# Spectral filter and SwiGLU on one core: the first filter load on SyncE, early fillers, a filter table of 33 slots, and another order of squares and sums

## The chip, the cores and the metric

The kernel runs on one core of one Trainium2 chip. Its time is the device time of one execution in microseconds; a kernel's time is the median over its runs. TensorE multiplies, VectorE and ScalarE (ACT) empty its PSUM banks, GpSimd (POOL) does elementwise work and issues DMAs, and SyncE (SP) only issues DMAs.

## The reference

```
X = rfft(x, axis=1)                    # x: 8 x 3008 x 256, along the 3008
Y = X * (filt_r + 1j * filt_i)         # 1505 frequencies x 256 channels
t = irfft(Y, n=3008, axis=1)           # 24064 tokens x 256
tn = t / sqrt(mean(t*t, -1) + 1e-6) * rms_g
g, val = tn @ w_gate, tn @ w_val       # 256 -> 1536
out = (g * sigmoid(g) * val) @ w_out   # 1536 -> 256
```
All inputs and the output are float32.

## The kernel before

**The transform.** 3008 is 47 x 64, so a transform is two stages of matmuls with constant tables: stage A over the 64 (table `wa`), stage B over the 47 (`wb`, one 96x96 block for each of 32 values of k2). The filter is multiplied in between B and its inverse (`wi`), and the inverse of A (`wai`) follows. Then each token is normed and goes through the gated layer: `gv` (gate and value, L545; Silu on ACT, product `hh` on VectorE) and `down` (L562).

**The filter table.** `ff` holds for each half `dh` of the channels and each k2 three sections of 48: minus imaginary, imaginary, real. The filters arrive in three loads of 512 rows (`f_load(i)`, filt_i as f=0 and filt_r as f=1, 512 KB each, on POOL's queue). `f_unit(i, f, dh, e)` transposes four 128x128 f32 blocks on TensorE (L390) and copies them into `ff` on engine `e`: 8 of 16 frequencies in rising k2, the other 8 mirrored, in four copies, because the mirror of k2=0 falls into another row. `f_neg(k0, n)` makes the minus section on POOL (L408) for both halves.

**The prologue, batch 0.** It is written out by hand, and each engine takes its instructions in the order written. `x_load(0, c)` are four loads on POOL; wa, ident, idf, wai and three tiny tails go on SyncE. `a0_unit` is stage A for four rows and one channel half (L359; psum on bank 1 for dh=0, emptied by ACT, bank 2 for dh=1, emptied by VectorE). `fill(n)` issues n matmuls on zeros whose result nobody reads (L425). `tr0_unit(g)` transposes stage A's result back (L369), eight times. Then a loop over 16 units (four k2 and one channel half each, unit i = 2g + dh) does stage B: `b_unit` (L243) and the two products `s_part` on VectorE (e=0 with the real section, L233; e=1 with the other two, L236), `yt0_unit` (sums the two products and transposes them on TensorE, L417, emptied by ACT), `bi_unit` (stage B's inverse, L287, emptied by ACT into `uu`, L197). After it `t4_load` moves `uu` by four transposing DMAs on SyncE (L301), `first_norm` norms the first tokens, and `n_first(1)` norms the second four rows from t4's first two chunks (L482).

POOL's queue in that time is: x(0), the filters, wb, wi, the weight loads `w_load(0)`, `w_load(1)`, then f_neg and `w_load(2)`, `wo_load`, the loads of x(1) and `w_gain` (weights times rms_g) in turn. `bank(i)` gives psum tiles: 0 is `mx` (one buffer), 1 `pg` and 2 `pv` (two buffers each, shared with gv), 3 `mb` (one buffer).

**The steady part.** 576 items (8 batches x 6 groups of rows x 12 blocks of 128 columns) each take one slot: `gv` of the slot, the planned units, `down` of the item two slots back. A planner places the units of the next batches: `a_unit` (stage A, bank 0 or 3, L208), `b_unit`, `s_part`, `add_unit` (sum of the products on POOL, L270), `yt_load` (transposing DMA, L277), `bi_unit`, `t4_load`, `n_unit` (L316), `sq_unit` (two squares with sums on ACT, L324), `stat_unit` and `xt_unit` (POOL, L332 to L342), `tr_unit` (transposing DMA). `fit` moves a unit to the first slot where its bank is free and ACT and VectorE have room by fixed costs. Within a slot units stand in the order in which they were planned, but what is in `front` is put first:

```python
        front = (sq_unit, s_part)
        def at(slot, fn, *a):
            todo = (late if fn == q_unit else plan).setdefault(slot, [])
            if fn in front:
                todo.insert(0, (fn, a))
            else:
                todo.append((fn, a))
```

Of the kernel before, what the change touches and what calls it, by code (L numbers as in the profile page):

```python
# [10 lines left out]
FP32 = mybir.dt.float32  # L11
# [9 lines left out]
P = 128  # L21
D = 256
# [3 lines left out]
H = 24  # L26
K2 = 32
SL = 48
# [6 lines left out]
NXC = H // XC  # L35
# [65 lines left out]
def kernel(  # L101
# [11 lines left out]
    nc = tc.nc  # L113
# [7 lines left out]
    if_d = nc.inline_tensor(if_np, name="if_t").ap()  # L121
# [3 lines left out]
    glob = ctx.enter_context(tc.tile_pool(name="glob", bufs=1))  # L125
# [25 lines left out]
    uu = glob.tile([P, H, 2, P], FP16)  # L151
    left = glob.tile([P, 2, K2, 2], FP16)
    va = uu.rearrange("p c e t -> p (c e t)").rearrange("p (e k j) -> p e k j", e=2, k=K2)
    ff = glob.tile([P, 2, K2, 3 * SL], FP32)
    wg = glob.tile([P, 2, DFF], FP16)
    wv = glob.tile([P, 2, DFF], FP16)
    wo = glob.tile([P, JT, D], FP16)
# [18 lines left out]
    def x_load(b, c):  # L176
        t = xp.tile([P, XC, D], FP16, tag="xc", name="xc")
        row = b * N + c * XC
        src = lambda n, w, lo=0: raw(x.flatten_outer_dims(), row + lo, [[N1 * D, n], [H * D, 2], [1, w * D]])
        if b == B - 1 and c == NXC - 1:  # L180
            w = XC - 1
            nc.vector.memset(t[96:P, w, :], 0.0)
            nc.gpsimd.dma_start(t[:, 0:w, :].rearrange("p a d -> p (a d)"), src(N2, w))
            nc.gpsimd.dma_start(t[0:P - 2, w, :], src(N2 - 1, 1, w))
            nc.gpsimd.dma_start(t[P - 2:P - 1, w, :],
                                raw(x.flatten_outer_dims(), row + w + (N2 - 1) * N1, [[D, 1], [1, D]]))
        else:
            nc.gpsimd.dma_start(t.rearrange("p a d -> p (a d)"), src(N2, XC))
        st[b]["x"][c] = t
# [5 lines left out]
    def copy(eng, out, in_, scale=None):  # L195
        if eng == "A":
            nc.scalar.activation(out=out, in_=in_, func=AXT.Copy, **({} if scale is None else {"scale": scale}))  # L197
        elif scale is None:
            nc.vector.tensor_copy(out=out, in_=in_)
        else:  # L200
            nc.vector.tensor_scalar(out=out, in0=in_, scalar1=scale, scalar2=None, op0=ALU.mult)
# [36 lines left out]
    def b_unit(b, i, bk=3):  # L238
        g, dh = divmod(i, 2)
        ps = bank(bk, "psb")[:, 0:4 * KR]  # L240
        for k in range(4):
            kk = 4 * g + k
            nc.tensor.matmul(ps[:, ts(k, KR)], st[b]["t2"][kk // KC][:, kk % KC, ds(dh * P, P)],  # L243
                             wb[0:KR, kk, :], start=True, stop=True)
        s = [sp.tile([P, 4, KR], FP16, tag="s%d" % e, name="s%d" % e) for e in range(2)]
        st[b]["s"][i] = (ps.rearrange("p (k r q) -> p k r q", k=4, r=2), s)
        s_part(b, i, 0)
# [127 lines left out]
    fst = {}  # L375
    FR4 = 4

    def f_load(i):
        t = stg.tile([P, 2, FR4, D], FP32, tag="stg", name="fs")
        fst[i] = t  # L380
        row = FR4 * P * i if i < 2 else NF - 1 - FR4 * P
        for f, src in ((0, filt_i), (1, filt_r)):
            nc.gpsimd.dma_start(t[:, f].rearrange("p a d -> p (a d)"),
                                raw(src, row, [[FR4 * D, P], [1, FR4 * D]]))

    def f_unit(i, f, dh, e):
        t = fst[i]
        ps = bank(1 + "AV".index(e), "psf").rearrange("p (a q) -> p a q", a=FR4)
        for a in range(FR4):
            nc.tensor.transpose(ps[:, a, :], t[:, f, a, ds(dh * P, P)], idf)  # L390
        v = ps.rearrange("p a (q s) -> p s a q", s=16)
        fk = ff[:, dh].rearrange("p (t k) c -> p t k c", k=4)
        lo = SL * (1 + f) + 8 * i
        hi = lo + H
        if i < 2:
            copy(e, fk[:, :, :, lo:lo + 8], v[:, 0:8])
            copy(e, fk[:, ::-1, 1:4, hi:hi + 8][:, :, ::-1, :], v[:, 8:16, 1:4, :])
            copy(e, fk[:, 1:8, 0, hi:hi + 8][:, ::-1, :], v[:, 9:16, 0, :])
            copy(e, ff[:, dh, 0, hi:hi + 8], v[:, 8, 0, :])
        else:  # L400
            copy(e, fk[:, :, :, lo:lo + 8], v[:, 8:16])
            copy(e, fk[:, ::-1, 1:4, hi:hi + 7][:, :, ::-1, :], v[:, 0:8, 1:4, 1:8])
            copy(e, fk[:, 1:8, 0, hi:hi + 7][:, ::-1, :], v[:, 1:8, 0, 1:8])
            copy(e, ff[:, dh, 0, hi:hi + 7], v[:, 0, 0, 1:8])

    def f_neg(k0, n):
        for dh in range(2):
            nc.gpsimd.tensor_scalar(out=ff[:, dh, k0:k0 + n, 0:SL], in0=ff[:, dh, k0:k0 + n, SL:2 * SL],  # L408
                                    scalar1=-1.0, scalar2=1.0, op0=ALU.mult, op1=ALU.mult)

# [11 lines left out]
    def fill(n, bk=0):  # L422
        ps = bank(bk, "pf")
        for _ in range(n):
            nc.tensor.matmul(ps, wa, ss3[0].rearrange("p k e q -> p (k e q)")[:, 0:512], start=True, stop=True)  # L425

    def t4_first():
        t = xtp.tile([P, 4, D], FP16, tag="xt", name="t4f")
# [160 lines left out]
    def w_load(q):  # L589
        cols = ts(q, DFF // 3)  # L590
        t = stg.tile([P, 2, 2, DFF // 3], FP32, tag="stg", name="ws")
        for src, k in ((moe_w_gate, 0), (moe_w_val, 1)):
            nc.gpsimd.dma_start(t[:, k], src.rearrange("(dt p) j -> p dt j", p=P)[:, :, cols])
        wst[q] = t

    def wo_load(q):
        nc.gpsimd.dma_start(wo[:, ts(q, JT // 3), :],
                            moe_w_out.rearrange("(jt p) d -> p jt d", p=P)[:, ts(q, JT // 3), :])

    def w_gain(q):  # L600
        cols = ts(q, DFF // 3)
        t = wst.pop(q)
        for k, dst in enumerate((wg, wv)):
            for dt_ in range(2):
                nc.gpsimd.tensor_scalar(out=dst[:, dt_, cols], in0=t[:, k, dt_, :],
                                        scalar1=gsb[:, dt_:dt_ + 1], scalar2=1.0,
                                        op0=ALU.mult, op1=ALU.mult)

    with tc.manual_schedule():
        nc.vector.memset(mhalf, -0.5)  # L610
        nc.vector.memset(epsb, 1e-6 * Y_SCALE * Y_SCALE)
        nc.scalar.activation(out=warm, in_=epsb.to_broadcast([P, 4]), func=AXT.Sqrt)
        for c in range(NXC):
            x_load(0, c)
        nc.sync.dma_start(wa, wa_d)
        nc.sync.dma_start(ident, id_d)
        nc.sync.dma_start(idf, if_d)
        nc.sync.dma_start(wai, wai_d)
        tail = op.tile([P, 4, D], FP32, tag="o3", name="tail")
        for f, src in ((0, filt_i), (1, filt_r)):  # L620
            nc.sync.dma_start(tail[0:1, f, :], raw(src, NF - 1, [[D, 1], [1, D]]))
        nc.sync.dma_start(tail[0:2, 2, 0:P], moe_rms_g.rearrange("(a p) -> a p", p=P))
        for i in range(3):
            f_load(i)
        for h in range(2):
            nc.gpsimd.dma_start(wb[:, ts(h, K2 // 2), :], wb_d[:, ts(h, K2 // 2), :])
        nc.gpsimd.dma_start(wi, wi_d)
        w_load(0)
        w_load(1)
        nc.vector.memset(ones, 1.0)  # L630
        for t in ss3:
            nc.vector.memset(t, 0.0)
        nc.vector.memset(ff.rearrange("p e k (s q) -> p e k s q", s=3)[:, :, 1:K2, :, SL - 1], 0.0)

# [2 lines left out]
        def a0(*gqs):  # L637
            for gq in gqs:
                for dh in range(2):
                    a0_unit(gq, dh, E[dh], 1 + dh)  # L640

        a0(0)
        fill(2)
        a0(1, 2)
        psg = bank(3, "psg")
        for f in range(2):
# [5 lines left out]
        copy("V", gsb, psg[:, 4:6])  # L652
        fill(2)
        a0(3)
        fill(1)
        a0(4, 5)
        todo = [(i, f, dh) for i in range(2) for f in range(2) for dh in range(2)]
        todo += [(2, f, dh) for dh in range(2) for f in range(2)]
        f_unit(*todo[0], "A")
        f_unit(*todo[1], "A")  # L660
        for g in range(8):
            tr0_unit(g, "V")
            if g < 7:
                f_unit(*todo[g + 2], "A")
        for n, u in enumerate(todo[9:]):
            f_unit(*u, "VAA"[n])
        f_neg(0, 8)
        w_load(2)
        f_neg(8, 8)
        wo_load(0)  # L670
        f_neg(16, 16)
        wo_load(1)
        wo_load(2)
        for c in range(NXC):
            x_load(1, c)
        for q in range(3):
            w_gain(q)
        UN = K2 // 2
        for p in range(UN + 3):
            if p < UN:  # L680
                b_unit(0, p, (0, 3)[p % 2])
                s_part(0, p, 1)
            if 2 <= p < UN + 1:
                yt0_unit(p - 2, "A", 1)
            if p == UN + 1:
                yt0_unit(UN - 1, "V", 1, slice(0, 2))
                yt0_unit(UN - 1, "A", 0, slice(2, 4))
            if 4 <= p < UN + 3:
                bi_unit(0, p - 4, "AV"[p == UN + 1], 2)
            if UN + 1 <= p < UN + 3:  # L690
                fill(1, 1)
        bi_unit(0, UN - 1, "V", 3, slice(0, 2))
# [6 lines left out]

        items = [(b, m, jt) for b in range(B) for m in range(6) for jt in range(JT)]  # L700
        plan, late = {}, {}
        front = (sq_unit, s_part)
        load = {r: [0.0] * (len(items) + 99) for r in "MBAV"}
        room = {"A": 0.8, "V": 0.7}
        for i in range(JT + 1, len(items), JT):
# [86 lines left out]
        for b in range(1, B):  # L792
# [18 lines left out]
            for m in range(6):  # L811
                norm_plan(b, m, (n_at + 8 * m, n_at + 8 * m + (4 if b > 1 else 2)), (2, 3, 7) if b > 1 else (2, 3, 6))

        stores = {}
        for i in range(len(items) + 4):
            if i < len(items):
# [46 lines left out]
```

## Time and profile before

| what | value |
|---|---|
| median of 3 runs | 869.14 us (869.07 to 870.27) |
| the profiled execution | 869.87 us, span 868.1 us |
| TensorE matmul, weight load | 852.2, 533.1 us busy |
| VectorE, ACT, POOL | 558.8, 614.5, 296.0 us busy |
| first matmul | 6.15 us |
| first matmul of gv | 45.39 us |

The span runs from the first instruction to the last; the execution's own time is 1.8 us longer. The span is cut by program order into the loads and stage A (to about 14.6 us), the filter transposes (to 23.7), the products (to 40.4), the first norm (to 45.4) and the 576 slots. In a timeline row the first number is the start, the second the length, both in us; merged rows give a count, and the time from one row's start to the next's is what the work cost where an engine is full. A bracket gives idle time before the row and what ended it.

### The profile page before, as it was taken

To read this page: it belongs to the slowest core of one execution; us is meant where nothing else is said; L and a number is where in the kernel's file an instruction comes from. 1 tells how busy PE (TensorE), PEld (TensorE's weight loads), DVE (VectorE), ACT (ScalarE), POOL (GpSimd) and SP (SyncE) were. 2 spreads that over 40 slices of the span, in tenths; PEclk is the share of its full clock that TensorE was granted. 3 is DMA by queue.
4 is the path that set the end of the run, shared out by engine and by line. 5 is a ranking of instruction groups with operands and counts; after the bars stand their busy time and mean duration, and the time that the engine had idled before them with its cause. 6 is when DMAs were issued, how large, how long until landed. Compare 5 with 4: busy or idle time off the path is not lost.

```text
span 868.1 us, 17009 instructions
## 1 busy us (share of the span) xinstructions
PE 852.2 (98%) x6127; PEld 533.1 (61%) x6127; DVE 558.8 (64%) x929; ACT 614.5 (71%) x1360; POOL 296.0 (34%) x341
## 2 busy tenths in 40 slices
PE   7999999999999999999999999999999999999997
PEld 6755666566665666666566666666666666665664
DVE  4856765776666666666676666667666766555554
ACT  5887787777578756877578865888567765777443
POOL 4814841453143322445025430443114440132000
PEclk9999999999999999999999999999999999999999
DMA  9986879755965576755656567534474431522201
GB/s 281 279 174 134 138 147 185 145 126 124 196 141 116 134 140 118 146 111 110 145 123 131 122 119 144 142 86 93 126 139 92 78 90 38 115 62 49 62 25 49
DMA packets 198621, 107.98 MB, mean 124 GB/s; under 512 B 158982, under 2 KB 182920, under 8 KB 198536
## 3 DMA queue, kind: packets, MB, share of 16 engines
q1 hardware_dynamic: 189896, 85.52, 44.9%
q0 software_dynamic: 8496, 21.24, 12.4%
q8 instruction: 48, 0.79, 0.4%
q14 instruction: 37, 0.30, 0.1%
q10 hardware_dynamic: 144, 0.13, 0.0%
HBM read 45.78 MB, written 35.65 MB: 94 GB/s over the span
## 4 chain that ended last, share of the span: by engine, by line
PE 93%; DMA 2%; ACT 2%; DVE 2%; issue 1%; POOL 0%; SPq 0%; DVEq 0%; POOLq 0%; ACTq 0%
PE po L562 27%; PE pg L545 27%; PE pv L545 26%; PE psb L243 3%; PE psi L287 2%; PE psn L316 2%; PE psa L208 2%; DVE hh L550 1%; ACT sg L549 1%; DMA yt<-ss 1%; DMA xc<-in_x_dram 1%; PE psf L390 1%; DMA t<-uu 1%; PE psy L417 1%; ACT uu L197 1%
## 5 line engine op out<-in xcount | busy, mean ns | idle before, releaser
L550 DVE TENSOR_TENSOR hh<-pv,sg 128x512 f16<-128x512 f32 (+2 forms) x578 | 392.0, 678 | 289.1 <-ACT sg L549 223.6
L549 ACT ACTIVATE sg<-pg 128x512 f16<-128x512 f32 (+2 forms) x578 | 338.0, 585 | 219.8 <-PE pg L545 215.3
L545 PE MATMUL pg<-xn,wg 128*128 128x512 f16 (+2 forms) x1156 | 337.9, 374 | 0.0
L545 PE MATMUL pv<-xn,wv 128*128 128x512 f16 (+2 forms) x1156 | 337.8, 374 | 0.0
L562 PE MATMUL po<-wo,hh 128*128 128x256 f16 x2256 | 332.7, 272 | 0.0
L562 PEld LDWEIGHTS <-hh 128*128 128x128 f16 x2256 | 213.5, 98 | 108.1 <-issue 4.8
L545 PEld LDWEIGHTS <-wv 128*128 128x128 f16 x1156 | 113.0, 98 | 130.6
L270 POOL TENSOR_TENSOR ss<-s,s 128x384 f16<-128x384 f16 x112 | 101.8, 910 | 247.6 <-DVE s L236 220.2
L545 PEld LDWEIGHTS <-wg 128*128 128x128 f16 x1156 | 111.5, 98 | 16.9 <-issue 0.2
L342 POOL TENSOR_TENSOR xt<-y,rho 128x1024 f16<-128x1024 f32 (+1 forms) x46 | 85.3, 1854 | 2.9
L324 ACT ACTIVATE junk<-y 128x256 f16<-128x256 f32 x180 | 74.5, 414 | 2.8
L233 DVE TENSOR_TENSOR s<-psb,ff 128x384 f16<-128x384 f32 x124 | 67.9, 548 | 0.6 <-PE psb L243 0.3
L236 DVE TENSOR_TENSOR s<-psb,ff 128x384 f16<-128x384 f32 x124 | 67.9, 547 | 0.0
L197 ACT ACTIVATE uu<-psi 128x384 f16<-128x384 f32 (+1 forms) x127 | 61.4, 485 | 1.9 <-PE psi L287 1.0
L197 ACT ACTIVATE y<-psn 128x512 f32<-128x512 f32 (+1 forms) x95 | 55.8, 588 | 4.1
L332 POOL TENSOR_SCALAR u<-ss 128x4 f32<-128x4 f32 (+1 forms) x46 | 8.9, 193 | 133.8 <-ACT junk L324 133.5
L287 PEld LDWEIGHTS <-yt 96*128 96x128 f16 x512 | 35.4, 97 | 27.5 <-DMA yt<-ss 1.1
L334 POOL TENSOR_TENSOR rho<-u,mhalf 128x4 f32<-128x4 f32 (+1 forms) x46 | 46.4, 1010 | 3.8
L197 ACT ACTIVATE t<-psa 128x512 f16<-128x512 f32 x71 | 42.1, 597 | 3.4 <-PE psa L208 1.7
L287 PE MATMUL psi<-wi,yt 96*128 96x96 f16 x512 | 42.9, 205 | 0.7 <-DMA yt<-ss 0.6
L243 PE MATMUL psb<-wb,t 96*128 96x96 f16 x480 | 40.1, 206 | 1.6 <-DVE s L236 1.3
L243 PEld LDWEIGHTS <-t 96*128 96x128 f16 x480 | 28.5, 98 | 14.6 <-DVE s L236 5.0
(97 smaller groups left out, 366.2 us busy)
## 6 DMA issues: line engine op xcount, KB each, us to landing
out_dram<-o SPq DMA_DIRECT2D x40, 512.0 KB, 3.6
xc<-in_x_dram POOLq DMA_DIRECT2D x31, 384.0 KB, 6.0
z_tmp<-t SPq DMA_DIRECT2D x28, 384.0 KB, 2.7
t<-z_tmp SPq DMA_DIRECT2D x28, 384.0 KB, 6.0
out_dram<-o SPq DMA_DIRECT2D x7, 384.0 KB, 2.7
fs<-in_filt_i_dram POOLq DMA_DIRECT2D x3, 512.0 KB, 11.0
fs<-in_filt_r_dram POOLq DMA_DIRECT2D x3, 512.0 KB, 11.0
ws<-in_moe_w_gate_dram POOLq DMA_DIRECT2D x3, 512.0 KB, 10.9
```

The costliest lines, as they stand in the source:

```text
L197: nc.scalar.activation(out=out, in_=in_, func=AXT.Copy, **({} if scale is None else {"scale": scale}))
L233: eng.tensor_tensor(out=o, in0=ps, in1=f1, op=ALU.mult)
L236: eng.tensor_tensor(out=o, in0=ps[:, :, ::-1, :], in1=f2, op=ALU.mult)
L243: nc.tensor.matmul(ps[:, ts(k, KR)], st[b]["t2"][kk // KC][:, kk % KC, ds(dh * P, P)], wb[0:KR, kk, :], start=True, stop=True)
L270: nc.gpsimd.tensor_tensor(out=ss3[g % 3][:, :, dh, 0:KR], in0=s[0], in1=s[1], op=ALU.add)
L287: nc.tensor.matmul(ps[:, k, :], yt[0:KR, k, dh, :], wi[0:KR, 4 * g + k, :], start=True, stop=True)
L324: nc.scalar.activation(out=junk, in_=y[:, i, ts(u, D)], func=AXT.Square, accum_out=ss[:, 2 * i + u:2 * i + u + 1])
L342: nc.gpsimd.tensor_tensor(out=xt[:, 0:n, :], in0=y.rearrange("p a (u d) -> p (a u) d", u=2)[:, 0:n, :], in1=rho[:, 0:n].unsqueeze(2).to_br ...
L545: nc.tensor.matmul(ps[:, 0:w], wt[:, dt_, ts(jt, P)], xn[:, q0:q1, dt_, :], start=(dt_ == 0), stop=(dt_ == 1))
L549: nc.scalar.activation(out=sg[:, c], in_=pg[:, 0:w], func=AXT.Silu)
L550: nc.vector.tensor_tensor(out=hh[:, c], in0=pv[:, 0:w], in1=sg[:, c], op=ALU.mult)
L562: nc.tensor.matmul(po[s4 // 2][:, s4 % 2, :], hh[:, ts(s4, P)], wo[:, jt, :], start=(jt == 0 and s4 % 2 == 0), stop=(jt == JT - 1 and (s4 ...
```

## The change

- **Loads.** `f_load` takes one filter and a queue. SyncE now issues idf first, then filt_i's first load, then wa, ident, wai and the tails; the other five filter loads stay on POOL.
- **Fillers.** `fill` multiplies zeros by zeros (`ss3[0]` is also the stationary operand), `ss3[0]` is zeroed first on VectorE, `fill(5)` stands ahead of everything on TensorE, and the counts between the a0 groups are 2, 3, 2, 4 instead of 0, 2, 2, 1. Two `fill(2, 2)` are new in the product loop.
- **Order of f_units.** The two of filt_i's first load go ahead of a0(0), those of filt_r's first load behind a0(4, 5), six between the tr0_units, f_unit(2, 0, 1) behind those and f_unit(2, 1, 1) behind the first b_unit. All are copied by ACT.
- **Table.** `ff` has 33 slots of k2, so that each f_unit makes two copies. The mirrored one writes to slots 1 to 32; `f_last` (POOL) copies slot 32 into slot 0.
- **Products.** `f_neg` can be called for one half; the units run in the order 2, 4, 3, 5, 6, 7, 0, 1, 8 to 15. f_neg(0, 4), f_neg(16, 16) and the loads behind them on POOL are written behind the first b_unit.
- **Steady part.** `add_unit` is put first in its slot too; and where the next slot has an a_unit on bank 0 and this one a bi_unit, the squares go last.

```diff
@@ -151,7 +151,7 @@
     uu = glob.tile([P, H, 2, P], FP16)
     left = glob.tile([P, 2, K2, 2], FP16)
     va = uu.rearrange("p c e t -> p (c e t)").rearrange("p (e k j) -> p e k j", e=2, k=K2)
-    ff = glob.tile([P, 2, K2, 3 * SL], FP32)
+    ff = glob.tile([P, 2, K2 + 1, 3 * SL], FP32)
     wg = glob.tile([P, 2, DFF], FP16)
     wv = glob.tile([P, 2, DFF], FP16)
     wo = glob.tile([P, JT, D], FP16)
@@ -375,12 +375,13 @@
     fst = {}
     FR4 = 4
 
-    def f_load(i):
-        t = stg.tile([P, 2, FR4, D], FP32, tag="stg", name="fs")
-        fst[i] = t
+    def f_load(i, f, eng):
+        if i not in fst:
+            fst[i] = stg.tile([P, 2, FR4, D], FP32, tag="stg", name="fs")
+        t = fst[i]
         row = FR4 * P * i if i < 2 else NF - 1 - FR4 * P
-        for f, src in ((0, filt_i), (1, filt_r)):
-            nc.gpsimd.dma_start(t[:, f].rearrange("p a d -> p (a d)"),
+        for src in ((filt_i, filt_r)[f],):
+            eng.dma_start(t[:, f].rearrange("p a d -> p (a d)"),
                                 raw(src, row, [[FR4 * D, P], [1, FR4 * D]]))
 
     def f_unit(i, f, dh, e):
@@ -389,22 +390,24 @@
         for a in range(FR4):
             nc.tensor.transpose(ps[:, a, :], t[:, f, a, ds(dh * P, P)], idf)
         v = ps.rearrange("p a (q s) -> p s a q", s=16)
-        fk = ff[:, dh].rearrange("p (t k) c -> p t k c", k=4)
+        fk = ff[:, dh, 0:K2].rearrange("p (t k) c -> p t k c", k=4)
+        fu = ff[:, dh, 1:K2 + 1].rearrange("p (t k) c -> p t k c", k=4)[:, ::-1, ::-1, :]
         lo = SL * (1 + f) + 8 * i
         hi = lo + H
         if i < 2:
             copy(e, fk[:, :, :, lo:lo + 8], v[:, 0:8])
-            copy(e, fk[:, ::-1, 1:4, hi:hi + 8][:, :, ::-1, :], v[:, 8:16, 1:4, :])
-            copy(e, fk[:, 1:8, 0, hi:hi + 8][:, ::-1, :], v[:, 9:16, 0, :])
-            copy(e, ff[:, dh, 0, hi:hi + 8], v[:, 8, 0, :])
+            copy(e, fu[:, :, :, hi:hi + 8], v[:, 8:16])
         else:
             copy(e, fk[:, :, :, lo:lo + 8], v[:, 8:16])
-            copy(e, fk[:, ::-1, 1:4, hi:hi + 7][:, :, ::-1, :], v[:, 0:8, 1:4, 1:8])
-            copy(e, fk[:, 1:8, 0, hi:hi + 7][:, ::-1, :], v[:, 1:8, 0, 1:8])
-            copy(e, ff[:, dh, 0, hi:hi + 7], v[:, 0, 0, 1:8])
-
-    def f_neg(k0, n):
+            copy(e, fu[:, :, :, hi:hi + 7], v[:, 0:8, :, 1:8])
+
+    def f_last():
+        v = ff.rearrange("p e k (s q) -> p e k s q", s=3)
         for dh in range(2):
+            nc.gpsimd.tensor_copy(out=v[:, dh, 0, 1:3, H:SL - 1], in_=v[:, dh, K2, 1:3, H:SL - 1])
+
+    def f_neg(k0, n, dhs=(0, 1)):
+        for dh in dhs:
             nc.gpsimd.tensor_scalar(out=ff[:, dh, k0:k0 + n, 0:SL], in0=ff[:, dh, k0:k0 + n, SL:2 * SL],
                                     scalar1=-1.0, scalar2=1.0, op0=ALU.mult, op1=ALU.mult)
 
@@ -422,7 +425,7 @@
     def fill(n, bk=0):
         ps = bank(bk, "pf")
         for _ in range(n):
-            nc.tensor.matmul(ps, wa, ss3[0].rearrange("p k e q -> p (k e q)")[:, 0:512], start=True, stop=True)
+            nc.tensor.matmul(ps, ss3[0][:, 0, 0, :], ss3[0].rearrange("p k e q -> p (k e q)")[:, 0:512], start=True, stop=True)
 
     def t4_first():
         t = xtp.tile([P, 4, D], FP16, tag="xt", name="t4f")
@@ -607,28 +610,32 @@
                                         op0=ALU.mult, op1=ALU.mult)
 
     with tc.manual_schedule():
-        nc.vector.memset(mhalf, -0.5)
+        nc.vector.memset(ss3[0], 0.0)
         nc.vector.memset(epsb, 1e-6 * Y_SCALE * Y_SCALE)
         nc.scalar.activation(out=warm, in_=epsb.to_broadcast([P, 4]), func=AXT.Sqrt)
         for c in range(NXC):
             x_load(0, c)
+        nc.sync.dma_start(idf, if_d)
+        f_load(0, 0, nc.sync)
         nc.sync.dma_start(wa, wa_d)
         nc.sync.dma_start(ident, id_d)
-        nc.sync.dma_start(idf, if_d)
         nc.sync.dma_start(wai, wai_d)
         tail = op.tile([P, 4, D], FP32, tag="o3", name="tail")
         for f, src in ((0, filt_i), (1, filt_r)):
             nc.sync.dma_start(tail[0:1, f, :], raw(src, NF - 1, [[D, 1], [1, D]]))
         nc.sync.dma_start(tail[0:2, 2, 0:P], moe_rms_g.rearrange("(a p) -> a p", p=P))
-        for i in range(3):
-            f_load(i)
+        f_load(0, 1, nc.gpsimd)
+        for i in range(1, 3):
+            for f in range(2):
+                f_load(i, f, nc.gpsimd)
         for h in range(2):
             nc.gpsimd.dma_start(wb[:, ts(h, K2 // 2), :], wb_d[:, ts(h, K2 // 2), :])
         nc.gpsimd.dma_start(wi, wi_d)
         w_load(0)
         w_load(1)
+        nc.vector.memset(mhalf, -0.5)
         nc.vector.memset(ones, 1.0)
-        for t in ss3:
+        for t in ss3[1:]:
             nc.vector.memset(t, 0.0)
         nc.vector.memset(ff.rearrange("p e k (s q) -> p e k s q", s=3)[:, :, 1:K2, :, SL - 1], 0.0)
 
@@ -639,8 +646,12 @@
                 for dh in range(2):
                     a0_unit(gq, dh, E[dh], 1 + dh)
 
+        fill(5)
+        for dh in range(2):
+            f_unit(0, 0, dh, "A")
+        fill(2)
         a0(0)
-        fill(2)
+        fill(3)
         a0(1, 2)
         psg = bank(3, "psg")
         for f in range(2):
@@ -652,41 +663,49 @@
         copy("V", gsb, psg[:, 4:6])
         fill(2)
         a0(3)
-        fill(1)
+        fill(4)
         a0(4, 5)
-        todo = [(i, f, dh) for i in range(2) for f in range(2) for dh in range(2)]
-        todo += [(2, f, dh) for dh in range(2) for f in range(2)]
-        f_unit(*todo[0], "A")
-        f_unit(*todo[1], "A")
+        for dh in range(2):
+            f_unit(0, 1, dh, "A")
+        todo = {g: (1, *divmod(g, 2)) for g in range(4)}
+        todo[4], todo[6] = (2, 0, 0), (2, 1, 0)
         for g in range(8):
             tr0_unit(g, "V")
-            if g < 7:
-                f_unit(*todo[g + 2], "A")
-        for n, u in enumerate(todo[9:]):
-            f_unit(*u, "VAA"[n])
-        f_neg(0, 8)
-        w_load(2)
-        f_neg(8, 8)
-        wo_load(0)
-        f_neg(16, 16)
-        wo_load(1)
-        wo_load(2)
-        for c in range(NXC):
-            x_load(1, c)
-        for q in range(3):
-            w_gain(q)
+            if g in todo:
+                f_unit(*todo[g], "A")
+        f_unit(2, 0, 1, "A")
+        f_neg(4, 4, (0,))
+        f_neg(8, 8, (0,))
+        f_neg(4, 4, (1,))
+        f_neg(8, 8, (1,))
         UN = K2 // 2
+        od = [2, 4, 3, 5, 6, 7, 0, 1] + list(range(8, UN))
         for p in range(UN + 3):
             if p < UN:
-                b_unit(0, p, (0, 3)[p % 2])
-                s_part(0, p, 1)
+                b_unit(0, od[p], (0, 3)[p % 2])
+                s_part(0, od[p], 1)
+            if p == 0:
+                f_unit(2, 1, 1, "A")
+                f_last()
+                f_neg(0, 4)
+                w_load(2)
+                wo_load(0)
+                f_neg(16, 16)
+                wo_load(1)
+                wo_load(2)
+                for c in range(NXC):
+                    x_load(1, c)
+                for q in range(3):
+                    w_gain(q)
+            if p < 2:
+                fill(2, 2)
             if 2 <= p < UN + 1:
-                yt0_unit(p - 2, "A", 1)
+                yt0_unit(od[p - 2], "A", 1)
             if p == UN + 1:
                 yt0_unit(UN - 1, "V", 1, slice(0, 2))
                 yt0_unit(UN - 1, "A", 0, slice(2, 4))
             if 4 <= p < UN + 3:
-                bi_unit(0, p - 4, "AV"[p == UN + 1], 2)
+                bi_unit(0, od[p - 4], "AV"[p == UN + 1], 2)
             if UN + 1 <= p < UN + 3:
                 fill(1, 1)
         bi_unit(0, UN - 1, "V", 3, slice(0, 2))
@@ -699,7 +718,7 @@
 
         items = [(b, m, jt) for b in range(B) for m in range(6) for jt in range(JT)]
         plan, late = {}, {}
-        front = (sq_unit, s_part)
+        front = (sq_unit, s_part, add_unit)
         load = {r: [0.0] * (len(items) + 99) for r in "MBAV"}
         room = {"A": 0.8, "V": 0.7}
         for i in range(JT + 1, len(items), JT):
@@ -811,6 +830,10 @@
             for m in range(6):
                 norm_plan(b, m, (n_at + 8 * m, n_at + 8 * m + (4 if b > 1 else 2)), (2, 3, 7) if b > 1 else (2, 3, 6))
 
+        for i, now in plan.items():
+            if any(fn == a_unit and a[3] == 0 for fn, a in plan.get(i + 1, ())) and bi_unit in [fn for fn, _ in now]:
+                now.sort(key=lambda u: u[0] == sq_unit)
+
         stores = {}
         for i in range(len(items) + 4):
             if i < len(items):
```

## The prediction

> **What bounds the kernel now.** I read the page's shares first, then the table by stage, the chain of waits at the start, and the timeline where TensorE starts late.
>
> ```profile
> PE 852.2 (98%) x6127; PEld 533.1 (61%) x6127; DVE 558.8 (64%) x929; ACT 614.5 (71%) x1360; POOL 296.0 (34%) x341
> ```
> ```profile
> 6.10:14.60 8.50, 8.40 (x60) 6.55 (x61) 3.63 (x8) 3.43 (x6) 2.68 (x5) 1.00 1.05 293
> 14.60:23.70 9.10, 9.10 (x115) 8.95 (x114) 6.71 (x12) 7.44 (x39) 3.40 (x5) 1.00 1.03 411
> 23.70:40.40 16.70, 15.28 (x257) 13.19 (x255) 16.03 (x37) 14.63 (x38) 16.14 (x25) 1.00 1.14 279
> ```
> TensorE is busy 98% of the span, so time can be won only where it idles, runs slowly, or does the prologue's own work. By stage (columns: length, then busy PE, PEld, DVE, ACT, POOL, clock, DMA share): to 14.6 us the x chunks and the clock bound it; to 23.7 TensorE does (9.10 of 9.10); to 40.4 VectorE does (16.03 of 16.70: the products); and the 16 DMA engines are full throughout (1.03 to 1.14).
>
> ```profile
> 2.05 6.20 DMA xc<-in_x_dram
> ...
> 22.44 1.32 PE psf L390 x12
> 23.75 0.18 PE psb L243 x4
> ...
> 24.06 0.10 DVE s L233
> ...
> 40.30 0.50 ACT uu L197
> ...
> 43.59 5.55 DMA t<-uu
> ```
> The chain runs from the x load through the filter transposes (psf) to the first product at 24.06, through the products, and then over the transposing load of t4, which TensorE meets at 49.18. From there its order is TensorE's own.
>
> ```profile
> 10.52 1.03 PE L425 MATMUL pf<-ss,wa 128*128 128x512 f16 x2
> 41.50 0.59 PE L425 MATMUL pf<-ss,wa 128*128 128x512 f16 x2
> ```
> The same two fillers take 1.03 us early and 0.59 late: TensorE starts at about half speed. The clock column says 1.00 in both, so durations must be read. Four 128-column f32 transposes take 0.44 us apart after 15 us; eight f16 ones are spaced 0.107 us at 12.63 and 0.056 in a tr0_unit.
>
> **Part 1, the loads.** filt_i's first 512 KB goes to SyncE, ahead of wa. No byte is added. One filter load is worth about 1.3 us of the full stream (POOL's issues released by landings stand at 13.40, 14.69, 15.96). Last landings of x are 11.8 (issue 3.11 + 8.7); they move up to 1.3 later, less the 0.4 us by which SyncE's data starts before POOL's: 12.7. From filt_r's first load on, the stream has as much ahead of it as before, so f1, f2 and wb come where they did or 0.4 earlier. wb's first half landed at 22.0 (issue 10.27 + 11.8): no product of batch 0 can start before 21.7. On SyncE's queue wa, ident, wai and the tails now stand behind idf and the filter; wai, fourth before, took 4.2 us from its issue at 2.09, so wa, third now, should land by 6.5, and x's first chunk, without which a0(0) can't start, not before 6.1 to 7.4.
>
> **Part 2, the clock.** ss3[0] is zeroed first (0.52 us, a third of 1.57), so five fillers of 0.43 us run from about 1.4 to 3.5. The first filter lands at about 4.9: 1.6 us from issue to data as for wa, then 1.3 to 2.6 for sharing with x (bounds 4.0 and 6.3). From there TensorE has no planned break. In half-speed time it has, up to the end of a0(4, 5): two f_units 1.7, eleven fillers 4.7, twelve a0_units of 0.43 5.1, psg 0.6, together 12.1; then nine f_units and eight tr0_units, 14.5. With full speed from T on, the first b_unit comes at T/2 + (4.9 + 26.6)/2 = T/2 + 15.75, not before 21.7. Before, full speed came 8.6 us after the first matmul (14.7 against 6.15), but 4.2 us after the last break (fillers at 10.52; one-column psg matmuls ahead of them). 8.6 gives T 13.5 and 22.5; 4.2 gives T 9.1 and the DMA bound, 21.7 to 22.0. I take 22.1, nearest to the unbroken row. The Trainium skill (TensorE: Matmul & The Clock Gate, Part 1) says that a fully busy window of about 3.4 us, running free of the kernel, raises the clock: by it the sum would be at the DMA bound.
>
> **Part 3, the filter table.** With 33 slots each f_unit makes two copies instead of four. ACT's four start 0.28, 0.21, 0.10 and 0.06 apart (0.64, from the 384 and 326 ns activations at 15.16 on); two of 256 elements are 0.56 if the doubly reversed one costs like the 32x8 one. Bounds: 0.50 and 0.64. It lies beside the 0.89 TensorE needs for an f_unit and a tr0_unit, so it is worth nothing; without that cover it is 0.08 per unit. f_last adds two tiny POOL copies, nearest the 0.46 us `left` copy, so at most 0.9, ahead of f_neg(0, 4), needed by the seventh unit some 5 us later.
>
> **Part 4, products by half.** Before, 12 f_units and 8 tr0_units stood between a0 and the products: the first b_unit came at 23.59, the first product at 24.06. Now two go ahead of a0 and one (f_unit(2,1,1)) behind the first b_unit: three times 0.44 less on the path. f_neg's 0.51 us splits and starts when filt_i's half is there; POOL's queue behind it (f_last, f_neg(0,4), w_load 1.5, wo_load 0.8, f_neg(16,16) 1.6) ends near 28.5, while unit 8 needs it at 30. The products go at 0.93 per unit, 16 of them, as before: VectorE sets it. The added f_unit and fillers (0.44 and 0.86) fit beside it. So the products start at 22.1 + 0.47 = 22.6 instead of 24.06 and end as much earlier: **1.5 us** (bounds 0.3 and 2.0).
>
> **Part 5, what is late next.** The t4 loads are issued 1.5 us earlier, at 39.6, while x(1, c) still fills the engines (DMA share 1.05 at 41, x landing to 44). TensorE wants t4's second chunk at n_first(1). Before it stood 0.45 us there. If the loads make half speed beside x they come in time (+0.45); if none, they land as before and 1.5 is lost. Between 43 and 44 us, with the last of x still moving, the engines carried 62 GB/s, and 249 in the next us, so I go below nothing: **-0.2 us**. The Trainium skill (DMA: Bandwidth & Descriptors, Queues, rings and completion order) says that an engine takes turns between its rings packet by packet; by that t4 gets its share beside x, this term is +0.45, and the sum would be 863.9.
>
> **Part 6, squares and sums.** The planner's arithmetic gives 14 slots in which a bi_unit with squares precedes an a_unit on `mx`; at 13 TensorE starts late. One of them, slots 136 and 137:
>
> ```profile
> 247.82 0.41 ACT L324 ACTIVATE junk<-y 128x256 f16<-128x256 f32 x1
> ...
> 248.77 0.47 ACT L197 ACTIVATE uu<-psi 128x384 f16<-128x384 f32 x1
> ```
> ```profile
> 247.56 0.34 PE L287 MATMUL psi<-wi,yt 96*128 96x96 f16 x4
> ...
> 248.60 0.59 PE L545 MATMUL pv<-xn,wv 128*128 128x512 f16 x2
> 249.29 0.38 PE L208 MATMUL psa<-xc,wa 128*128 128x512 f16 x1
> ```
> psi is done at 247.90, but its copy waits behind two squares until 248.77; TensorE could start psa at 248.60 + 0.43 = 249.03 and starts at 249.29, 0.26 late. With the copy first it ends by 248.4 and the wait is gone; ACT's total is unchanged and the squares' users (stat_unit, xn) are slots away. In the timeline the same place shows six times 0.255 (249 to 292), twice 0.41 (356, 361) and five times 0.09 (346 to 397): 1.53 + 0.82 + 0.44 = **2.8 us**. add_unit goes ahead of xt_unit on POOL:
>
> ```profile
> 404.57 1.89 POOL L342 TENSOR_TENSOR xt<-y,rho 128x1024 f16<-128x1024 f32 x1
> 406.42 0.91 POOL L270 TENSOR_TENSOR ss<-s,s 128x384 f16<-128x384 f16 x1
> ```
> The yt load waits for that sum and is issued 1.85 us earlier now; psi at 413.76 stood 0.76 us for yt (ready at 412.57 + 0.43). That is **0.7**. xt, and after it xn, come 0.9 later with many slots to spare. For new small waits I take off 0.2: **3.3 us** (bounds 2.0 and 3.9).
>
> **Sum.** 1.5 - 0.2 + 3.3 = 4.6. The profiled execution took 869.87 for a span of 868.1; the runs' median is 869.14. So 865.3 by that execution's own time, and 864.5 as a median.
>
> **Rivals.**
> First, the prologue's gain is eaten: t4 waits for the x stream, or T is late. For it: the 62 GB/s above. Then only Part 6 is left, 3.3: 865.8. Chance 0.18.
> Second, Part 6 fails: the bank wait returns at the next copy, as ACT's work is conserved. Against it: ACT stood 0.88 us for pg just before 247.33, so it has room. Only the prologue then: 867.8. Chance 0.08.
> Third, slower: the clock. If zeros do not count as work for the clock and the full rate comes late, every us of T beyond 15.7 costs half a us; at T = 22.3 it outweighs Part 6, at 25.8 it is slower by 0.2%; if it came only with the products they would start at 31.5, 7.9 later, and the time would be 873.7. Against it: the fillers of before streamed zeros too, and full speed came at 14.7 through one of them. Chance 0.06.
> Fourth, the change does not do what it says: wb's landing slips by the 1.3 us and the table's merged copies cost more, while Part 6 stalls merely move: about 869. Chance 0.04.
>
> **Numbers.** The forecast has 0.64. About 0.2% (1.74 us, 867.4) is what a measurement of this kernel can tell from no change. The range takes the bounds 0 to 2.0 of the prologue and 2.0 to 3.9 of Part 6, 5.9 to 2.0 us, and the spread of the runs (869.07 to 870.27): 862.9 to 867.4. Faster: forecast, first rival and a share of the second, 0.84; same 0.09; slower 0.07.
>
> **What would show it.** Right: first b_unit at about 22, first product near 22.6, 0.93 per unit after it; first gv matmul near 43.9 (45.39 before); fillers spaced 0.22 by 12 us; no wait of psa on ACT between 245 and 400; the yt load of the 244th slot ahead of xt. Wrong: psn at n_first waiting 1 us or more for t4, psa waiting as before, a0(4, 5) ending after 15, or VectorE idle between products because f_neg is late.

## The result and the profile after

The changed kernel takes 865.28 us as the median of six runs (865.13 to 866.43); the kernel before 869.27 beside it (six runs, 869.06 to 870.53). The ratio is 0.9953, with a 95% interval of 0.9941 to 0.9966: 4.0 us, or 0.46%, less. The profiled execution took 865.26 us for a span of 863.5. Here and below a ratio leaves out single executions over 1.5% above the fastest of their kernel, which a median keeps, so the two can differ.

The page's shares (busy us and share of the span):

```profile
PE 852.5 (99%) x6142; PEld 533.2 (62%) x6142; DVE 556.9 (64%) x925; ACT 613.7 (71%) x1340; POOL 296.8 (34%) x344
```
TensorE is as busy as it was, with 15 matmuls more, in a span 4.6 us shorter: what went was its idle time.

TensorE's own timeline, at the places that the prediction named:

```profile
1.45 2.32 PE L428 MATMUL pf<-ss 128*128 128x512 f16 x5 [1.45 <-DVE epsb L614]
5.11 1.94 PE L391 MATMUL psf<-idf,fs 128*128 128x128 f32 x8 [1.35 <-DMA fs<-in_filt_i_dram]
...
11.38 0.22 PE L660 MATMUL psg<-idf,tail 2*128 2x2 f32 x1 [0.85 <-DMA tail<-in_moe_rms_g_dram]
11.53 0.61 PE L428 MATMUL pf<-ss 128*128 128x512 f16 x2
...
22.08 0.34 PE L243 MATMUL psb<-wb,t 96*128 96x96 f16 x4
...
43.91 0.38 PE L548 MATMUL pg<-xn,wg 128*128 128x256 f16 x2
```
filt_i's first load lands at 5.0, two fillers take 0.61 by 11.5 (1.03 before, at 10.52), the first b_unit stands at 22.08 instead of 23.59, and gv starts at 43.91 instead of 45.39. New is the wait of 0.85 for the last tail.

```profile
42.16 6.04 DMA t<-uu
48.20 0.05 issue
48.24 0.40 PE psn L485 x4
```
The chain of waits still crosses t4's second load; it now takes 6.04 us from its issue (5.55 before). Then slots 136 and 137, ACT first, TensorE second:

```profile
246.96 0.49 ACT L197 ACTIVATE uu<-psi 128x384 f16<-128x384 f32 x1
247.35 0.41 ACT L324 ACTIVATE junk<-y 128x256 f16<-128x256 f32 x1
```
```profile
247.63 0.59 PE L548 MATMUL pv<-xn,wv 128*128 128x512 f16 x2
248.06 0.38 PE L208 MATMUL psa<-xc,wa 128*128 128x512 f16 x1
```
The copy goes ahead of the squares, and psa starts 0.43 after pv, with no wait. On POOL the sum now precedes xt:

```profile
401.11 0.91 POOL L270 TENSOR_TENSOR ss<-s,s 128x384 f16<-128x384 f16 x1 [0.35 <-DVE s L236]
401.98 1.89 POOL L342 TENSOR_TENSOR xt<-y,rho 128x1024 f16<-128x1024 f32 x1
```
The start of every slot's first gv matmul in both traces, subtracted, gives where the span's 4.6 us went: -1.48 at the first slot; -0.94 from the third on (0.54 given back at n_first(1)); -3.74 after the 240th, in 13 steps, each behind a re-sorted slot; -4.51 at the 251st, where psi had waited for yt; -4.61 at the end.

### The profile page after: what moved, and what is told of

Read it like the earlier page. It is cut to its first block, busy times and chain, and to the rows that moved or that the text cites. A ratio compares the mean times of both kernels' runs of the same rounds, so it can differ in the third digit from the quotient of the medians.

```text
span 863.5 us, 17023 instructions
## 1 busy us (share of the span) xinstructions
PE 852.5 (99%) x6142; PEld 533.2 (62%) x6142; DVE 556.9 (64%) x925; ACT 613.7 (71%) x1340; POOL 296.8 (34%) x344
## 4 chain that ended last, share of the span: by engine, by line
PE 95%; DMA 2%; DVE 1%; ACT 1%; SPq 0%; issue 0%
PE po L565 28%; PE pg L548 28%; PE pv L548 28%; PE psb L243 3%; PE psi L287 2%; PE psn L316 2%; PE psa L208 2%; DMA tail<-in_moe_rms_g_dram 1%; DMA t<-uu 1%; PE psy L420 1%; PE psf L391 0%; PE pst L369 0%; DVE s L233 0%; DVE s L236 0%; DVE hh L553 0%
## 6 DMA issues: line engine op xcount, KB each, us to landing
ws<-in_moe_w_gate_dram POOLq DMA_DIRECT2D x3, 512.0 KB, 11.5
ws<-in_moe_w_val_dram POOLq DMA_DIRECT2D x3, 512.0 KB, 11.7
```

## The experiments

All are compared with the kernel before, run beside them on the same chip (medians 869.0 to 869.27). "Third slot" is the start of the gv matmul behind n_first(1). From there to the last slot the other nine profiles below gain 3.54 to 3.59 on the first one where Part 6 is in, and at most 0.19 where it isn't. Full speed is the change of the clock in the trace's record, seen in the matmuls' spacing.

| run | full speed, us | gv, us | third slot, us | median, us | ratio, 95% interval |
|---|---|---|---|---|---|
| before, first profile | 14.7 | 45.39 | 49.85 | 869.27 | 1 |
| before, second profile | 11.6 | 44.08 | 49.27 | 869.24 (one run) | |
| changed | 8.4 | 43.91 | 48.91 | 865.28 | 0.9953 (0.9941 to 0.9966) |
| Part 6 alone | 11.7 | 44.20 | 49.31 | 865.75 | 0.9964 (0.9951 to 0.9977) |
| prologue alone | 7.8 | 44.71 | 49.47 | 868.82 | 0.9998 (0.9989 to 1.0007) |
| no fill(5) | 8.8 | 43.89 | 48.75 | 865.67 | 0.9961 (0.9947 to 0.9975) |
| no fillers to a0(4, 5) | 17.0 | 45.31 | 49.85 | 866.69 | 0.9973 (0.9963 to 0.9983) |
| first load back on POOL | 5.4 | 44.28 | 48.84 | 865.62 | 0.9959 (0.9946 to 0.9971) |
| four copies | 9.8 | 44.98 | 48.99 | 865.47 (of four, one at 3926.22) | 0.9958 (0.9942 to 0.9973) |
| tails behind wa | 9.3 | 43.94 | 48.60 | 865.07 | 0.9953 (0.9940 to 0.9967) |

**The steady part without the prologue.**

```diff
-        front = (sq_unit, s_part)
+        front = (sq_unit, s_part, add_unit)
...
+        for i, now in plan.items():
+            if any(fn == a_unit and a[3] == 0 for fn, a in plan.get(i + 1, ())) and bi_unit in [fn for fn, _ in now]:
+                now.sort(key=lambda u: u[0] == sq_unit)
```


> The kernel before with Part 6 alone (add_unit in front, squares last where an a_unit on mx follows). Theory: the three terms are independent, so the 13 bank waits (2.80 us) and the wait for yt at the 250th slot (0.77) go as they did in the changed kernel: 3.6 us less than before, 865.7 as a median; gv starts at 45.4 as before. Rival: the waits had their place because of the prologue's timing, and half of it stays: under 2 us less.

Measured: 865.75, the forecast median, though 3.25 below the 869.0 beside it and not 3.6. From the third slot to the end it loses the same steps as the changed kernel: -0.54 to -3.32 up to the 240th slot (2.78), then 0.77 at the 251st. The rival falls: the waits belong to the planner's order. What was not expected is that gv starts at 44.20 instead of 45.39, though nothing ahead of it was edited.

**The prologue without the steady part.**

```diff
-        front = (sq_unit, s_part, add_unit)
+        front = (sq_unit, s_part)
...
-        for i, now in plan.items():
-            if any(fn == a_unit and a[3] == 0 for fn, a in plan.get(i + 1, ())) and bi_unit in [fn for fn, _ in now]:
-                now.sort(key=lambda u: u[0] == sq_unit)
```


> The changed kernel with before's front and no sort: the prologue alone. Theory: gv starts 1.5 us earlier, n_first(1) gives 0.5 of it back waiting for t4, nothing else: 0.9 less than before, 868.3. Rival: the prologue's shift also moves the POOL and DMA order of the first slots, and what is lost or won there shows in the slots after the third: over 0.3 off.

Measured: 868.82 (868.28 to 870.36), and the interval of the ratio holds 1: of the whole prologue no gain can be told. The theory's 868.3 is missed by 0.5, and its rival falls too, as behind the third slot no lasting step is over 0.15. In this execution the tails came later than in the changed kernel's:

```profile
11.21 0.28 PE L659 MATMUL psg<-idf,tail 1*128 1x1 f32 x2 [1.11 <-DMA tail<-in_filt_i_dram]
11.73 0.28 PE L659 MATMUL psg<-idf,tail 1*128 1x1 f32 x2 [0.23 <-DMA tail<-in_filt_r_dram]
12.22 0.22 PE L660 MATMUL psg<-idf,tail 2*128 2x2 f32 x1 [0.21 <-DMA tail<-in_moe_rms_g_dram]
```
Three waits of 1.55 us together delay stage A; gv starts at 44.71, and the third slot at 49.47.

**A second profile of the kernel before** (no edit).

> The kernel before, unchanged, for a second profile. Theory: the execution first profiled had a late clock (full speed at 14.7 us), which alone put its products 1.2 us later than in the run of Part 6 alone (full speed at 11.7); in another execution full speed may come earlier and gv then starts between 44.2 and 45.4, with a time of 868.7 to 869.9 that goes with it. Rival: 14.7 is this prologue's rule, and the run of Part 6 was the exception.

Measured: 869.24 (span 867.4), full speed at 11.6, gv at 44.08, 0.1 ahead of the theory's stretch. The rival falls. So the first profile, 869.87, was of an execution with a late clock, and gv's start moves by 1.3 us between executions of one program. About half of it reaches the end:

```profile
48.60 0.40 PE L482 MATMUL psn<-wai,t 128*128 128x128 f16 x4 [1.01 <-DMA t<-uu]
49.27 0.59 PE L545 MATMUL pg<-xn,wg 128*128 128x512 f16 x2
```
TensorE waits 1.01 us for t4 at n_first(1), and the third slot starts at 49.27, only 0.58 earlier; the span is 0.67 shorter.

**The fillers.** First those ahead of the filter alone, then all 16 up to a0(4, 5).

```diff
-        fill(5)
         for dh in range(2):
             f_unit(0, 0, dh, "A")
```


> The changed kernel without the five fillers ahead of the first filter transposes. Theory: what raises the clock is the unbroken work from 5.1 us on, so full speed still comes near 8.4 to 9, and the time is that of the changed kernel within 0.2. Rival: the zeros from the first us raise it; then the fillers between the a0 groups run at 0.43 until some 12 us, and the first product is 0.3 to 1 later.

Measured: 865.67 (864.86 to 865.88, against 865.13 to 866.43), full speed at 8.8, the first b_unit at 22.06. In this place the five fillers from the first us do nothing that these runs show.

```diff
-        fill(5)
         for dh in range(2):
             f_unit(0, 0, dh, "A")
-        fill(2)
         a0(0)
-        fill(3)
         a0(1, 2)
...
-        fill(2)
         a0(3)
-        fill(4)
         a0(4, 5)
```


> The changed kernel without any filler up to a0(4, 5) (16 fewer). Theory: TensorE then has a break ahead of each x chunk, unbroken work begins with a0(4, 5) near 13, full speed comes between 16.5 and 20, and the first b_unit at T/2 + 14.65, 22.9 to 24.6 instead of 22.1: 0.8 to 2.5 us slower than the changed kernel. Rival: the loads bound it (x to 13.0, wb to 21.9) and the clock is worth nothing: within 0.3.

Measured: 866.69, 1.4 above the changed kernel and inside the theory's 0.8 to 2.5; full speed at 17.0, first b_unit at 23.48 (T/2 + 14.65 = 23.1). The eight executions (866.11 to 867.51) overlap only with the slowest of the changed kernel's six, 866.43, and the third slot comes 0.94 later. So the fillers between the loads are worth their place; that it is by leaving TensorE no breaks fits the theory's formula, but rests on one profile.

**The filter's first load back on POOL, its f_units behind a0(4, 5).**

```diff
-        f_load(0, 0, nc.sync)
...
-        f_load(0, 1, nc.gpsimd)
-        for i in range(1, 3):
+        for i in range(3):
...
-        for dh in range(2):
-            f_unit(0, 0, dh, "A")
         fill(2)
         a0(0)
...
-        for dh in range(2):
-            f_unit(0, 1, dh, "A")
+        for f in range(2):
+            for dh in range(2):
+                f_unit(0, f, dh, "A")
```


> The changed kernel with filt_i's first load back on POOL's queue behind x(0) and its two f_units behind a0(4, 5). Theory: x, wa and the tails land 1.2 us earlier, so stage A ends near 13, but two f_units more (0.89) stand ahead of the products, and the clock rises later, as work starts at 6.2: first b_unit 22.0 to 23.2, the time 0 to 1 us above the changed kernel's. Rival: the load on SyncE is where the prologue's gain comes from, and undoing it costs 1.2 or more.

Measured: 865.62 (865.32 to 866.21), 0.3 above the changed kernel with overlapping ranges. gv starts 0.38 later, the third slot 0.07 earlier. So the move to SyncE is not where a gain comes from. The theory's clause on the clock was wrong: full speed came at 5.4, earliest of all, and ahead of that TensorE had run nothing but seven fillers:

```profile
1.45 3.38 PE L428 MATMUL pf<-ss 128*128 128x512 f16 x7 [1.45 <-DVE epsb L614]
...
6.76 0.81 PE L428 MATMUL pf<-ss 128*128 128x512 f16 x3
```
The seven stand 0.43 apart up to 4.8, the next three 0.22. So zeros times zeros raise the clock by themselves.

**Four copies per f_unit, 32 slots.** Edit: `ff`, `f_unit` and `f_neg`'s surroundings as in the kernel before, no `f_last`.

```diff
-    ff = glob.tile([P, 2, K2 + 1, 3 * SL], FP32)
+    ff = glob.tile([P, 2, K2, 3 * SL], FP32)
...
-                f_last()
```


> The changed kernel with the table of 32 slots: four copies per f_unit again and no f_last. Theory: ACT's copies lie beside TensorE's 0.89 per pair, so the time is that of the changed kernel within 0.2. Rival: ACT is the one that TensorE follows there (0.64 and more per unit with its fixed cost), and the products start 0.3 to 1 later.

Measured: 865.47, the same as the changed kernel. f_units and tr0_units follow each other at 0.44 as with two copies. This execution again had late tails, and gv at 44.98; yet the third slot is at 48.99:

```profile
48.11 0.61 PE L483 MATMUL psn<-wai,t 128*128 128x128 f16 x8
48.99 0.59 PE L546 MATMUL pg<-xn,wg 128*128 128x512 f16 x2
```
gv came 1.08 us later than in the changed kernel, and the third slot 0.08 later: TensorE just did not wait for t4. In five programs with gv between 43.89 and 44.98 (changed, no fill(5), first load back, four copies, tails) the third slot lies between 48.60 and 48.99. The prologue alone, with gv between these too, has it at 49.47. What orders all six is x(1): its last chunk landed at 43.79 to 44.09 in the five and at 44.66 in the sixth, and t4's second chunk 4.10 to 4.14 us behind it in each.

**Tails behind wa.**

```diff
         nc.sync.dma_start(wa, wa_d)
+        tail = op.tile([P, 4, D], FP32, tag="o3", name="tail")
+        for f, src in ((0, filt_i), (1, filt_r)):
+            nc.sync.dma_start(tail[0:1, f, :], raw(src, NF - 1, [[D, 1], [1, D]]))
+        nc.sync.dma_start(tail[0:2, 2, 0:P], moe_rms_g.rearrange("(a p) -> a p", p=P))
         nc.sync.dma_start(ident, id_d)
         nc.sync.dma_start(wai, wai_d)
```


> The changed kernel with the three tiny tail loads issued on SyncE right behind wa, ahead of ident and wai. Theory: the psg transposes wait 0.85 to 1.55 us for tails queued behind 512 KB of filter and the tables; earlier tails free stage A, which then ends on x's last chunk (13.0 + 0.9), 0.2 to 1.0 earlier, and the first b_unit comes at 21.9 (wb) instead of 22.1 to 22.9: 0.2 to 0.8 us less. Rival: the tails are slow for their own sake (single rows), and move with the queue, no gain.

Measured: 865.07 (865.02 to 865.46). The waits at psg are gone, but the first b_unit stands at 22.10, where it was: TensorE next waits 0.3 for x and 0.4 for filt_r, which is behind x in the stream. The best of the runs, 0.2 below the changed kernel, which these runs can't tell from none.

**t4 by itself.** Three forms: loads that need not be there early are held on POOL behind a tiny copy that waits for the first norm (first and second run) or for t4's fourth chunk (third and fourth).

```diff
-                wo_load(1)
-                wo_load(2)
-                for c in range(NXC):
+                for c in range(2):
                     x_load(1, c)
...
         first_norm()
+        nc.gpsimd.tensor_copy(out=hold, in_=st[0]["xn"][0][:, 0, 0, 0:2])
+        wo_load(1)
+        x_load(1, 2)
+        wo_load(2)
+        x_load(1, 3)
```


> The changed kernel with two wo loads and x(1)'s last two chunks (6.4 us of the stream) issued only after the first norm, so that t4's first two chunks move by themselves. Theory: TensorE's wait at n_first(1) comes from t4 sharing the engines with x; t4's second chunk then lands near 44 instead of 48.2, the step from gv to the third slot is 0.5 us shorter, and the time 0.4 to 0.6 less than the changed kernel's. Rival: the transposes are slow by themselves or held by their issue on SyncE (2.5 us each), and the wait stays; or the later x chunks make a_unit wait at the sixth to ninth slot.

Measured: 878.02, ratio 1.0086 (1.0061 to 1.0110). Its profiled execution took 1278.47 us at a granted clock of 0.66 and is not read; of the other eight, one took 868.66. The second run is this edit with the tails' edit:

> The changed kernel with both edits: tails behind wa, and t4 by itself. Theory: the two gains add, as one lies ahead of the products and one behind them: 0.6 to 1.4 us less than the changed kernel. Rival: an earlier start of the products is lost again at wb or at t4, and no more than the larger of the two is left.

Measured: 877.61, ratio 1.0064 (1.0032 to 1.0095), eleven executions from 864.81 to 879.25, the profiled one 878.08. What was wanted came first: gv at 44.07, the third slot at 48.08, 4.0 us apart. Then, among the longest waits from 44 to 75 us:

```profile
ACT t L198 <- DMA z_tmp<-t: 12.0, 1, 12.0
...
PE psa L209 <- ACT t L198: 8.5, 1, 8.5
```
A store of z_tmp from 51.28 takes 19.9 us, and ACT can't empty the next psa until it frees its tile. The table of the same run (DMA share and GB/s are the last two columns):

```profile
45.00:46.00 1.00, 1.00 (x6) 0.42 (x5) 0.76 (x2) 1.00 (x4) 1.00 (x3) 1.00 1.10 247
46.00:54.00 8.00, 8.00 (x60) 4.75 (x59) 3.43 (x6) 7.35 (x14) 2.33 (x4) 1.00 1.31 158
```
At 45 to 46 t4 moves alone, at 247 GB/s (287 in the next run, at 46 to 47). With the held loads beside t4's third and fourth chunks the engines stay full (1.31) and move 158 in the mean, from 79 to 265 in single us. In the packets of 50.5 to 51.5 us there are 43 of t4 (256 bytes) beside 31 of x (3 KB). That the store crawls for the same reason is not shown.

The times of these two runs go with the mean granted clock: 864.81 and 868.66 have 1.000 and 0.999, all others 0.991 to 0.995 (1278.47 apart). In the profiled execution the clock reads 0.63 at 60 to 70 us and 0.68 at 70 to 80, where TensorE stands in this stall and starts again. So the long executions are, by their clock, those with such a stall, and some have none. With the hold at t4's fourth chunk:

```diff
-        nc.gpsimd.tensor_copy(out=hold, in_=st[0]["xn"][0][:, 0, 0, 0:2])
+        nc.gpsimd.tensor_copy(out=hold, in_=st[0]["t4"][3][:, 0, 0:2])
+        x_load(1, 2)
         wo_load(1)
-        x_load(1, 2)
-        wo_load(2)
         x_load(1, 3)
+        wo_load(2)
```


> As the run in which t4 moved alone, but the held loads wait for t4's fourth chunk, in the order x, wo, x, wo. Theory: the stall of that run came from t4's third and fourth chunks and the z_store behind them in SyncE's queue crawling beside x; with all four ahead they land by 47, TensorE doesn't wait at n_first(1), nor at the ninth slot, and gv to the third slot takes 4.0 us instead of 5.0: 0.8 to 1.0 less than the changed kernel, 864.4. Rival: the held loads come too late for the sixth slot (x) or for down (wo), and TensorE waits there as long or longer.

Measured: 870.75, ratio 1.0012 (1.0003 to 1.0021). The third slot stands at 48.08 again, 0.83 earlier than in the changed kernel. Then the rival decides:

```profile
50.07 0.18 POOL L717 COPY hold<-t 128x2 f16<-128x2 f16 x1 [10.01 <-DMA t<-uu]
```
```profile
55.46 0.39 PE L209 MATMUL psa<-xc,wa 128*128 128x512 f16 x1 [1.40 <-DMA xc<-in_x_dram]
57.98 0.60 PE L566 MATMUL po<-wo,hh 128*128 128x256 f16 x4 [2.13 <-DMA wo<-in_moe_w_out_dram]
```
t4's fourth chunk lands at 50.0, not 47, and the held x and wo are missing when their slots come: 3.9 us given back for 0.83. (The profiled execution took 868.34; most of the eleven took 2 us more, at a mean granted clock of 0.996 to 0.998 instead of 0.999.) So it is shown that holding back x's last two chunks (with two wo loads) ends the wait at n_first(1); that it can be had for free is not. Holding only x(1)'s last chunk was not tried.

Sharing with x is not all of that wait. In the changed kernel x's last chunk lands at 44.09, and then t4, alone, stops for more than a us:

```profile
44.50:44.75 0.25, 0.25 (x5) 0.23 (x3) 0.00 (x0) 0.24 (x3) 0.00 (x0) 1.00 1.27 289
...
45.50:45.75 0.25, 0.25 (x3) 0.10 (x2) 0.25 (x1) 0.25 (x2) 0.00 (x0) 1.00 0.63 4
...
46.25:46.50 0.25, 0.25 (x3) 0.12 (x2) 0.17 (x1) 0.17 (x2) 0.00 (x0) 1.00 0.08 9
...
47.00:47.25 0.25, 0.25 (x4) 0.15 (x4) 0.02 (x1) 0.25 (x1) 0.00 (x0) 1.00 1.27 290
```
Ahead of it stands one 16 KB packet of queue q8, which the page calls instruction; it starts at 44.84 and takes 1.16 us. In every trace but that of 1278 us, thirteen of them, such a packet meets t4, at 43.1 to 47.3 us, and some 0.5 to 1 us after its start t4 falls under 20 GB/s for 0.75 to 1.5 us. The changed kernel's three earlier ones (19.4, 27.8 and 35.5), beside ordinary loads, leave no such gap. The gap is longer than the wait of 0.74 at n_first(1). No run moves that packet by itself, so its part in the wait is not shown by an experiment.

The fourth run adds the tails' edit and moves f_units:

```diff
-        for dh in range(2):
-            f_unit(0, 1, dh, "A")
...
             tr0_unit(g, "V")
+            if g == 0:
+                for dh in range(2):
+                    f_unit(0, 1, dh, "A")
```


> The last one, with the tails behind wa and the two f_units of filt_r's first load behind the first tr0_unit. Theory: tr0_unit(0) fills the 0.4 us in which TensorE waits for filt_r (landing at 14.3), and the products start 0.3 earlier, bound then by wb at 21.7: 0.2 to 0.4 less than the run before it, about 864.1. Rival: wb or the copies of tr0_unit on VectorE bind first: no difference.

Measured: 871.23, ratio 1.0024 (1.0013 to 1.0035). The first b_unit is at 23.43, not earlier: tr0_unit(0) now stands ahead and waits 0.5 us for ACT's copy of stage A and 0.2 for VectorE's, and an f_unit 0.3 for ACT; the held wo and x cost 3.5 again. A miss.

## Why the prediction was right

**Part 6** carried it. 2.8 us at 13 places and 0.7 for yt were forecast; the traces show 2.80 and 0.77, slot by slot, and Part 6 alone gives 865.75 against 865.7. The allowance of 0.2 for new small waits was not needed: 3.57 instead of 3.3.

**Part 4's end of the chain** came out as 1.48 for 1.5, first product 22.51 for 22.6, products at 0.93. Against the first profile the sum stands: -4.61 for 4.6, and the same execution's 869.87 - 4.6 = 865.3 is the measured 865.28. For the prologue's share that is luck: it holds against an execution with a late clock, and only there.

**The step that was off** is the last one, the median. The sum was made against an execution 0.7 us above the median, and taken from the median all the same: 864.5, 0.8 too low. Most of the excess was a late clock (the second profile is 0.63 shorter), which is what the prologue's edits remove, so it was counted twice. Against the second profile (full speed at 11.6) the first b_unit gains 0.21, gv 0.17 and the third slot 0.36. "8.6 us after the first matmul" in Part 2 was one execution's number. The range, too, doesn't follow from its terms: 5.9 to 2.0 us off 869.07 to 870.27 is 863.2 to 868.3, not 862.9 to 867.4; the result lies in both.

**Part 5 was mis-sized**: 0.54 for 0.2. It is also more than a loss to be taken off. With x(1) in the stream to 44 us, t4's second chunk lands near 48, with the changed prologue 4.1 us behind x's last chunk; gv's start hardly reaches the end. This fits the ratio of 0.9998 for the prologue alone, and that Parts 1 to 3, undone one at a time, showed nothing outside the ranges, except all fillers together (1.4). Part 4's order was not undone by itself. The first rival, a prologue gain eaten by t4 with Part 6 left (865.8), describes the mechanism better than the forecast's own middle, which lies between. The Trainium skill's page DMA: Bandwidth & Descriptors, Queues, rings and completion order, says that engines take turns packet by packet. The 43 packets of t4 beside 31 of x agree roughly; the 339 beside 15 at 42 to 43 us in the changed kernel don't. What the prediction drew from it, that t4 comes in time (+0.45), was wrong, and turns don't show why: at 43 to 44 the engines were busy for 0.30 of the time and moved 52 GB/s, and at 45 to 47 t4 had them to itself and moved 86 and 70.

**The clock.** Part 2 chose between 4.2 and 8.6 us of work to full speed; it came 3.3 us after the first filter transpose (8.4 against 5.1), and 2.7 to 5.7 in the eight profiles that start on the filter with these fillers behind it, so the shorter row was right. x's last chunk landed at 13.0 for 12.7, and wa at 7.2 for 6.5. What bound the rest was not wb, as Parts 1 and 2 had it: filt_r's first load lands at 14.3, f_unit(0, 1) starts at 14.43, and 17 units of 0.45 from there give 22.1, just after wb at 21.9. With the tails behind wa, wb landed at 21.7 and the first b_unit stayed at 22.10. The slower rival, that zeros do not count for the clock, falls with the run of the first load back on POOL, where seven fillers alone brought full speed at 5.4. **Part 3** is worth nothing, as forecast.

## What to carry to other kernels

Look for the wait that is repeated where a planner repeats: thirteen waits of 0.08 to 0.41 us, which hardly show in the list of waits, were worth more than the whole hand-made prologue, and reordering two instructions within a slot removed them for nothing. Before a prologue is shortened, follow the chain to the next transfer that all of it must meet: here much of a gain ahead of a full DMA stream ended there. And a sum made against one execution must be applied to that execution; where its time is above the median, ask whether the excess is the thing that the change removes.

## What was not expected of the hardware

A transposing load in 256-byte packets beside ordinary loads moved 79 to 265 GB/s with them, 158 in the mean, with an engines' share of 1.31; the transposes alone ran at 247 to 290 GB/s, x alone at 209 (41 to 42 us in the kernel before). Behind a 16 KB packet of the instruction queue, and with no other load beside them, the transposes fell from 289 to at most 10 GB/s between 45.5 and 46.75 us in the changed kernel, and under 20 for 0.75 to 1.5 us in the twelve other traces. Matmuls of zeros with zeros raised TensorE's clock: seven of them, from 1.45 to 4.83 us, and full speed at 5.36. The time to full TensorE speed differed between executions of one program by 3.1 us (11.6 and 14.7). The eleven times of the run with both edits spread over 14 us and go with the stall behind z_tmp; what decides whether it comes, 864.8 or 879, stays open.
